# A two-layer decode kernel: VectorE turns x and q between the layers, an eleventh K tile stays in SBUF, and the pieces around the turn are cut anew

## The chip, the cores and the metric

The kernel runs on 1 core of one Trainium2 chip. The time is device microseconds of one execution; of several runs the median is given. The profile is of one execution.

## The reference

Two identical layers of decoding for B = 4 rows of D = 512 floats. Each layer is attention over a cache (32 query heads in 8 groups of 4, 4096 cached positions of 128 floats), then a gated feed-forward of width 1792. Everything is fp32. Both layers use the same cache and the same weights.

```python
x = A_x
for _ in range(2):
    h = layernorm(x)                        # (h - mean) / sqrt(var + 1e-5)
    q = (h @ wq).reshape(4, 1, 32, 128)     # 4 query heads to each of 8 cache heads
    p = softmax(q @ k_cache.T * 128 ** -0.5)
    x = x + (p @ v_cache).reshape(4, 1, 4096) @ wo
    h = layernorm(x)
    x = x + (silu(h @ w1) * (h @ w3)) @ w2
```

## The kernel before, in words

**Tiles.** For one cache head the K and V of all four rows are cut into 32 tiles of 128 partitions by 4 KB (0.524 MB each): tiles 0 to 15 are K (two halves of eight), 16 to 31 are V (two halves of eight). A head is done in four stages on TensorE: `score` of the first half (L391, two matmuls a tile), `score` of the second, `weigh` of the first half of V (L450, two matmuls a tile), `weigh` of the second. DVE takes the maxima (L403), ACT the exponentials (L407), TensorE turns the result (L414). The output of one head is turned and multiplied by its part of wo during the next head's first scores (`turn_o` after four tiles, `gather_o` after six).

**Order of the heads.** Layer 0 takes heads 0 to 7, layer 1 takes 7 to 0. Head 7 is thus used twice in a row, and a part of it stays in SBUF over the feed-forward: the K tiles in `KEPT` (6 to 15), and of tiles 0 and 1 three quarters, which ACT puts into three PSUM banks (`stored`) and back.

**The ring.** `space` holds 216 KB in each partition. wq and wo of all heads lie at fixed places from 96 KB up (`at_wq`, `at_wo`; 8 KB each) and are given back head by head in layer 1 (`vacate`). All else is a ring, handed out when the program is built: `plan` lists the pieces in the order of their transfers, `pump` issues the next piece as soon as `take` finds a place for it, and `done` gives a piece's place back when the last of its tiles has been read, in the program's order. `take` is first-fit: the lowest hole that is long enough, between the two limits that `narrow` sets. One piece needs one hole in one stretch. The plan is strictly in order: a piece that finds no place holds up all behind it.

```python
for i, (at, size) in enumerate(free):
    a, b = max(at, low, limit[0]), min(at + size, limit[1])
    if b - a >= n:
```

On the chip the issue (SP, L217; L205 for weights at fixed places, L215 for the rest of tile 1) waits by semaphores for the reads and the earlier transfers of those bytes. Transfers take eight semaphores in turn (DMAHW0 to DMAHW7).

`PARTS` says how many tiles each piece of K and V has, for every layer and head. For layer 1 these are: head 6 (3, 2, 2, 5, 4, 7, 9), head 5 (10, 8, 7, 7), head 4 (7, 1, 13, 11), and so on; a piece of 10 tiles is 40 KB in each partition.

**The turn.** At the end of layer 0, w1 lies at 0 to 28 KB (two pieces, L205), the kept tiles above it, wq and wo above 96 KB, and w3, w2 and the first pieces of layer 1 pass through what is left: 28 to 56 KB, a ring of 28 KB. Between w2's last matmul (L567) and the first score of layer 1 the chain is: add x and sum its rows (DVE, L581), mean (TensorE, L308), turn x (TensorE, L316 and L317; ACT copies, L320), q = x wq (L352, which also gives wq's place back), scale by 1/std (DVE, L356; the power by GpSimd, L332), turn q (TensorE, L357), lay it out (DVE, L342).

Of the kernel before, what the change touches and what calls it, by code (L numbers as in the profile page):

```python
# [14 lines left out]
LAYERS = 2  # L15
# [36 lines left out]
TURN = HKV - 1  # L52
KEPT = range(6, 16)
STORED = 0
# [4 lines left out]
PARTS = [{0: (16, 16), 1: (16, 16), 2: (16, 16), 3: (10, 7, 7, 8), 4: (16, 9, 7), 5: (8, 10, 7, 7), 6: (11, 13, 8),  # L59
# [4 lines left out]


W2_PARTS = ((0, 2), (2, 4), (4, 6), (6, 8), (8, 10), (10, 12), (12, 13), (13, 14))
BUSY = (4, 1, 2, 2, 1)
# [7 lines left out]
def tile_decode_layers(ctx: ExitStack, tc: tile.TileContext, x, kv, wqo, wo0, w1, w3, w2, out):  # L75
# [58 lines left out]
    def keep(at, n, src, given=None):  # L134
        plan.append((None, src, (at, n, (at, n) if given is None else given)))
# [16 lines left out]
    def w1_load():  # L152
        for k, n in ((0, 3), (3, 1)):
            keep(k * F // KB, n * F // KB, w1[:, k * F:(k + n) * F])

# [3 lines left out]
    for layer in range(LAYERS):  # L159
# [26 lines left out]
        for u in range(2):  # L186
            for k in (0, 2):
                a = 4 * KC * FW[0] * u + 4 * FW[u] * k
                stream([("w3", layer, u, k), ("w3", layer, u, k + 1)], w3[:, a:a + 8 * FW[u]])
        for a, b in W2_PARTS:  # L190
            stream([("w2", layer, a)], w2[:, a * D:b * D])

# [63 lines left out]
    nc.vector.tensor_scalar(same, same, -1.0 / D, None, op0=ALU.mult)  # L256
    spare = const.tile([P, 1], F32, name="spare")
    half = const.tile([P, 1], F32, name="half")
    nc.vector.memset(half, -0.5)


# [48 lines left out]

    def layernorm(xin, rowsum):
        busy(BUSY[2])
        pt = turned()
        at = [o_ps[1][:, i:i + 1] for i in range(2)]
        mean(at[0], rowsum)
        nc.tensor.matmul(pt[:, 0, :], xin, ident, start=True, stop=False)  # L316
        nc.tensor.matmul(pt[:, 0, :].rearrange("p (k c) -> p k c", k=KC), rowsum.to_broadcast([P, P]),  # L317
                         same.rearrange("p (k c) -> p k c", k=KC), start=False, stop=True)
        xT = work.tile([P, P], F32, name="xT", bufs=1)
        nc.scalar.activation(xT, pt[:, 0, :], AF.Copy)  # L320
        xc = work.tile([P, P], F32, name="xc", tag="tmp", bufs=1)
        nc.vector.tensor_scalar(xc, xin, at[0], None, op0=ALU.add)
# [3 lines left out]
        rstd = small("rstd")  # L326

        def factor():
            mean(at[1], ssq)
            ve = small("ve")  # L330
            nc.vector.tensor_scalar(ve, at[1], EPS, None, op0=ALU.add)
            nc.gpsimd.tensor_tensor(rstd, ve, half, op=ALU.pow)  # L332

        return xT, rstd, factor

# [9 lines left out]
    def wq_of(g):  # L345
        return place(at_wq(g), HOME).rearrange("p (k n) -> p k n", k=KC)

    def project_q(layer, g, xT, rstd):
        w = wq_of(g)
        for k in range(KC):  # L350
            for h in range(REP):
                nc.tensor.matmul(misc[32 * h:32 * h + 32, :], xT[:, 32 * k:32 * k + 32],  # L352
                                 w[:, k, h * DH:(h + 1) * DH], start=(k == 0), stop=(k == KC - 1))
        vacate(at_wq(g))
        q = work.tile([P, DH], F32, name="q", tag="tmp", bufs=1)
        nc.vector.tensor_scalar(q, misc, rstd, SCALE, op0=ALU.mult, op1=ALU.mult)  # L356
        nc.tensor.transpose(misc, q, ident)  # L357
        copy_q(misc.rearrange("p (h b) -> p b h", h=REP)[:, 0:B, :])

# [41 lines left out]

    def maximum(i, ps, acc):
        nc.vector.tensor_reduce(acc[:, i:i + 1], ps, axis=AX.X, op=ALU.max, negate=True)  # L403

    def exponent(i, ps, acc):
        p = work.tile([P, NT, P], F32, name="p", bufs=1)
        nc.scalar.activation(p.rearrange("p n s -> p (n s)"), ps, AF.Exp, bias=acc[:, i:i + 1],  # L407
                             accum_out=acc[:, 2 + i:3 + i])
        return p
# [103 lines left out]

    def feed_forward(layer, xT, rstd, factor, rowsum):
        pg = o_ps[0]
# [17 lines left out]
        gate = work.tile([P, FJ], F32, name="gate", tag="p", bufs=1)  # L533
        nc.scalar.activation(gate, pg[:, 0:FJ], AF.Sigmoid, scale=rstd)
        nc.scalar.activation(spare, half, AF.Exp)
        nc.vector.scalar_tensor_tensor(gate, pg[:, 0:FJ], rstd, gate, op0=ALU.mult, op1=ALU.mult)
        pt = turned()

        def hidden(u):
            s = slice(FW[0] * u, FW[0] * u + FW[u])  # L540
            nc.vector.scalar_tensor_tensor(gate[:, s], sides[u][:, 0:FW[u]], rstd, gate[:, s], op0=ALU.mult, op1=ALU.mult)

# [19 lines left out]
        def down():  # L562
            for i, (a, b) in enumerate(W2_PARTS):
                t = loaded("w2", layer, a).rearrange("p (n e) -> p n e", n=b - a)
                for m in range(a, b):
                    for k in range(KC):
                        nc.tensor.matmul(x_ps[32 * k:32 * k + B, :], hT[:, m, :],  # L567
                                         t[:, m - a, k * P:(k + 1) * P], start=(m == 0), stop=(m == 13))
                done("w2", layer, a)
                if i == 0:  # L570
                    turn_h(1)

        up(0, range(KC))
        hidden(0)
        up(1, (0, 1))
# [3 lines left out]
        down()  # L579
        if layer < LAYERS - 1:  # L580
            nc.vector.scalar_tensor_tensor(x_sb, x_ps, 1.0, x_sb, op0=ALU.mult, op1=ALU.add,  # L581
                                           accum_out=rowsum)
        else:
            nc.vector.tensor_tensor(x_sb, x_ps, x_sb, op=ALU.add)

    rowsum = small("rowsum")
    nc.vector.reduce_sum(rowsum, x_sb, axis=AX.X)
    for layer in range(LAYERS):
        xT, rstd, factor = layernorm(x_sb, rowsum)
        order = orders[layer]  # L590
        factor()
        if layer:
            project_q(layer, order[0][0], xT, rstd)
        else:
            share_q(layer, order[0][0], xT)
            turn_q(take_q(rstd))
            copy_q()

        ready = HKV - 3 if layer == 0 else HKV - 2
        between = {}  # L600
        for n, (g, (first, last)) in enumerate(order):
            acc = work.tile([P, 24], F32, name="acc")
            ps = score(layer, g, first, between)
            maximum(0, ps, acc)
            if n + 1 < len(order):
                share_q(layer, order[n + 1][0], xT)
            p = exponent(0, ps, acc)
            pT = turn(p)
            between = {}
            if n + 1 < len(order):  # L610
                shares = take_q(rstd)
                between[2] = lambda shares=shares: turn_q(shares)
            if n > ready:
                between[4] = lambda n=n: add_o(take_o(gathered if n == ready + 1 else wide))
            ps = score(layer, g, last, between)
            maximum(1, ps, acc)
            p = exponent(1, ps, acc)
# [10 lines left out]
        nc.scalar.activation(spare, half, AF.Sigmoid)  # L628
# [5 lines left out]
        xT, rstd, factor = layernorm(x_sb, rowsum)  # L634
        rowsum = small("rowsum")
        feed_forward(layer, xT, rstd, factor, rowsum)
    nc.sync.dma_start(out, x_sb)

# [43 lines left out]
```

## Time and profile before

| | |
|---|---|
| median of 3 runs | 709.15 us (708.6 to 709.89) |
| the profiled execution | 707.68 us |
| its span | 705.9 us |
| read from HBM | 298.65 MB, 423 GB/s over the span |
| busy: TensorE, VectorE, ScalarE, GpSimd | 61%, 20%, 6%, 0% of the span |
| mean granted TensorE clock | 0.823 |

The span is the profiled part of the execution; 1.8 us lie around it. "SPq" rows are issues of transfers. In a row of the timeline the two numbers ahead are start and length in us; the bracket behind is how long the engine had been idle before it, and what ended that. fp32 matmuls stand as two instructions each (x32 is 16 matmuls), and two matmuls on different column groups run side by side.

### The profile page before, as it was taken

The numbers are of one execution on the slowest core, as the hardware profiler recorded it, in microseconds if no ns is written. First come the engines' busy times: TensorE is split into PE (matmuls) and PEld (weight loads), VectorE is DVE, ScalarE is ACT, GpSimd is POOL, SyncE is SP. The second block draws the span as 40 slices with busy tenths as digits, with TensorE's granted clock in tenths as the row PEclk, the third lists the DMA queues.
The fourth block names the chain that finished last, engine by engine and source line by source line (L and its number), as shares of the span: only waits on it lengthen the run. The fifth ranks groups of instructions, "written<-read, shape, count | busy, mean of one in ns | idle before, by whom it ended". The sixth has DMA issues, their size and how long they took to land.

```text
span 705.9 us, 7248 instructions
## 1 busy us (share of the span) xinstructions
PE 431.1 (61%) x3161; PEld 134.6 (19%) x3161; DVE 142.1 (20%) x500; ACT 42.4 (6%) x101; POOL 2.9 (0%) x10
## 2 busy tenths in 40 slices
PE   3515734648526677466777857585386573566777
PEld 2101201212102122121224212121121121121223
DVE  3102102103201213031121301212112121212231
ACT  0000000100001000001111101010000101000011
POOL 0000000000000000000000000000000000000000
PEclk9977767859868769798899978799768987788898
DMA  9999999999999999999999999999999999999997
GB/s 420 416 417 431 450 420 418 467 411 424 452 408 431 443 420 431 446 413 424 424 412 411 403 430 440 429 426 431 437 431 435 422 451 428 442 428 412 421 419 279
DMA packets 15151, 299.18 MB, mean 424 GB/s; under 512 B 1680, under 2 KB 1936, under 8 KB 5392
## 3 DMA queue, kind: packets, MB, share of 16 engines
q1 hardware_dynamic: 14976, 298.65, 99.1%
q8 instruction: 25, 0.41, 0.2%
q10 hardware_dynamic: 144, 0.07, 0.0%
q14 instruction: 6, 0.05, 0.0%
HBM read 298.65 MB, written 0.07 MB: 423 GB/s over the span
## 4 chain that ended last, share of the span: by engine, by line
DMA 74%; PE 21%; another core or an unknown queue 2%; DVE 1%; ACT 1%; issue 1%; SPq 0%; ACTq 0%; DVEq 0%
DMA space<-in_kv 67%; PE scores L391 11%; DMA space<-in_w 8%; PE o L450 6%; PE sums_ps L375 1%; PE stored L501 1%; PE turned L414 1%; ACT p L407 1%; DVE acc L403 0%; PE sums_ps L567 0%; PE sums_ps L473 0%; PE o L523 0%; PE scores L300 0%; PE sums_ps L352 0%
## 5 line engine op out<-in xcount | busy, mean ns | idle before, releaser
L391 PE MATMUL scores<-space,qT 128*32 128x512 f32 x1024 | 176.2, 737 | 119.2 <-DMA space<-in_kv 118.7
L450 PE MATMUL o<-space,pT 128*16 128x512 f32 x1024 | 156.0, 706 | 118.4 <-DMA space<-in_kv 108.9
L391 PEld LDWEIGHTS scores<-space,qT 128*32 128x32 f32 x1024 | 37.0, 126 | 203.5 <-issue 185.1
L450 PEld LDWEIGHTS o<-space,pT 128*16 128x16 f32 x1024 | 31.5, 108 | 222.4 <-DMA space<-in_kv 125.8
L407 ACT ACTIVATE p<-scores,acc 128x512 f32<-128x512 f32 x32 | 22.0, 687 | 575.9 <-DVE acc L403 442.3
L403 DVE TENSOR_REDUCE acc<-scores 128x1 f32<-128x512 f32 x32 | 22.1, 691 | 156.0 <-PE scores L391 151.4
L416 DVE COPY pT<-turned 128x256 f32<-128x256 f32 x32 | 13.6, 424 | 186.8 <-PE turned L414 186.8
L463 DVE SCALAR_TENSOR_TENSOR o<-o,acc,o 128x128 f32<-128x128 f32 x112 | 39.3, 351 | 43.3 <-PE o L450 39.9
L414 PE MATMUL turned<-ident,p 128*128 128x128 f32 x128 | 23.5, 312 | 13.2 <-ACT p L407 13.2
L474 DVE COPY oT<-sums_ps 128x16 f32<-128x16 f32 x16 | 2.8, 174 | 109.0 <-PE sums_ps L473 109.0
L414 PEld LDWEIGHTS turned<-ident,p 128*128 128x128 f32 x128 | 15.0, 153 | 45.3 <-ACT p L407 28.0
L363 PE MATMUL sums_ps<-space,xT 128*32 128x512 f32 x120 | 19.1, 656 | 2.9 <-DMA space<-in_wqo 2.7
L375 PEld LDWEIGHTS sums_ps<-same,shares 128*128 128x128 f32 x120 | 17.0, 218 | 16.6 <-DVE shares L370 9.4
L375 PE MATMUL sums_ps<-same,shares 128*128 128x4 f32 x120 | 18.3, 276 | 1.0 <-DVE shares L370 1.0
L501 PE MATMUL stored<-space,oT 128*32 128x512 f32 x104 | 14.4, 593 | 0.0
L567 PE MATMUL sums_ps<-space,hT 128*4 128x128 f32 x224 | 9.5, 285 | 5.4 <-DMA space<-in_w 5.4
L370 DVE TENSOR_SCALAR shares<-sums_ps,rstd 128x512 f32<-128x512 f32 x15 | 11.1, 743 | 2.0 <-PE sums_ps L363 2.0
L473 PEld LDWEIGHTS sums_ps<-head,o 128*128 128x128 f32 x32 | 6.0, 233 | 22.0 <-issue 18.3
L523 PE MATMUL o<-space,xT 128*32 128x192 f32 (+1 forms) x128 | 7.3, 356 | 3.2 <-DMA space<-in_w 3.2
L300 PE MATMUL scores<-ident 128*128 128x256 f32 (+2 forms) x22 | 8.1, 451 | 1.4 <-POOL ident masks.py:199 1.4
L473 PE MATMUL sums_ps<-head,o 128*128 128x16 f32 x32 | 7.6, 314 | 1.2 <-DVE o L463 1.2
L529 PE MATMUL o<-space,xT 128*32 128x448 f32 x64 | 6.8, 545 | 1.1 <-DMA space<-in_w 0.7
(95 smaller groups left out, 135.3 us busy)
## 6 DMA issues: line engine op xcount, KB each, us to landing
space<-in_kv SPq DMA_DIRECT2D x11, 3584.0 KB, 20.7
space<-in_kv SPq DMA_DIRECT2D x7, 4096.0 KB, 22.2
space<-in_kv SPq DMA_DIRECT2D x4, 5632.0 KB, 22.9
space<-in_kv SPq DMA_DIRECT2D x4, 5120.0 KB, 20.0
space<-in_kv SPq DMA_DIRECT2D x14, 1024.0 KB, 11.5
space<-in_kv SPq DMA_DIRECT2D x2, 6656.0 KB, 23.7
space<-in_wqo SPq DMA_DIRECT2D x3, 4096.0 KB, 39.5
space<-in_kv SPq DMA_DIRECT2D x2, 4608.0 KB, 18.0
```

What stands on the lines that cost most here:

```text
L363: nc.tensor.matmul(wide[32 * k:32 * k + 32, :], xT[:, 32 * k:32 * k + 32], w[:, k, :], start=True, stop=True)
L370: nc.vector.tensor_scalar(shares, wide, rstd, -D * SCALE, op0=ALU.mult, op1=ALU.mult)
L375: nc.tensor.matmul(misc[:, h * B:(h + 1) * B], shares[:, h * DH:(h + 1) * DH], same[:, 0:B], start=True, stop=True)
L391: nc.tensor.matmul(ps[32 * b:32 * b + 32, :], qT[:, b, at:at + 32], t[:, i * BLOCK:(i + 1) * BLOCK], start=(m < 2), stop=(m >= TILES - 2))
L403: nc.vector.tensor_reduce(acc[:, i:i + 1], ps, axis=AX.X, op=ALU.max, negate=True)
L407: nc.scalar.activation(p.rearrange("p n s -> p (n s)"), ps, AF.Exp, bias=acc[:, i:i + 1], accum_out=acc[:, 2 + i:3 + i])
L414: nc.tensor.transpose(pt[:, n, :], p[:, n, :], ident)
L416: nc.vector.tensor_copy(pT, pt.rearrange("p n (b r) -> p n b r", b=B)[:, :, :, 0:ROW])
L450: nc.tensor.matmul(o_ps[i][32 * b:32 * b + ROW, :], pT[:, r // 2, b, :], t[:, j * NB * DH:(j + 1) * NB * DH], start=(r < 2), stop=(r >= TI ...
L463: nc.vector.scalar_tensor_tensor(o, o_ps[s][:, j * DH:(j + 1) * DH], acc[:, 16 + NB * s + j:17 + NB * s + j], o, op0=ALU.mult, op1=ALU.add)
L473: nc.tensor.matmul(misc[:, 0:B * REP], o, head, start=True, stop=True)
L501: nc.tensor.matmul(bank[32 * h:32 * h + 32, :], oT[:, h, :], w[:, h, :], start=first, stop=last)
```

## The change

- `KEPT` is tiles 5 to 15: eleven K tiles of head 7 (44 KB) stay over the turn, and layer 1 loads 0.524 MB less. The ring at the turn is 28 to 52 KB: 24 KB.
- Head 7's pieces in both layers are cut anew, finer in V and at the start of layer 1. The lists of all other heads are as before.
- w1 comes as 20 and 8 KB (21 and 7 before). At the turn w3's first half comes in four pieces of 4 KB (two of 8), its second half in two of 6 KB as before. At the end of layer 1 w3 comes in two pieces (16 and 12 KB; four before) and w2 in five (8, 8, 6, 4, 2 KB; eight before).
- At the turn DVE turns x straight from PSUM (in blocks of 32 by 32; the rows of wq, w1 and w3 are laid out to match) and turns q; x is added to w2's sums by a matmul with the identity; the scaling by 1/std is left to the scores of that head (`maximum` and `exponent` take a scale). So that q needs no mean, wq of head 7 is centred in place during head 5 of layer 0 (`center`: four matmuls and one DVE add).

```diff
-KEPT = range(6, 16)
+KEPT = range(5, 16)
...
-          7: ((6, 28), (2, 28), (8, 28), (2, 24), (6, 0), (4, 32), (2, 32), (2, 24))},
+          7: ((5, 32), (3, 52), (8, 64), (2, 20), (5, 0), (1, 28), (4, 32), (1, 48), (2, 20), (1, 28))},
...
-          7: (((2, 2), 2), ((3,), 24), None, ((1, 2, 2), 27), ((2, 2, 2, 2), 16))}]
-W2_PARTS = ((0, 2), (2, 4), (4, 6), (6, 8), (8, 10), (10, 12), (12, 13), (13, 14))
+          7: (((2, 1), 2), ((2, 1), 24), None, ((1, 2, 2), 27), ((2, 2, 2, 2), 16))}]
+W1_PARTS = (20, 8)
+W3_PARTS = (((1, 1, 1, 1), (2, 2)), ((4,), (4,)))
+W2_PARTS = ((2, 2, 2, 2, 2, 2, 1, 1), (4, 4, 3, 2, 1))
...
+    def lay_down(xin):
         xT = work.tile([P, P], F32, name="xT", bufs=1)
-        nc.scalar.activation(xT, pt[:, 0, :], AF.Copy)
+        nc.vector.transpose(xT, xin)
+        return xT
...
+    def center(g):
+        w = wq_of(g)
+        for k in range(KC):
+            nc.tensor.matmul(stored[1], share.to_broadcast([P, P]), w[:, k, :], start=(k == 0), stop=(k == KC - 1))
+        nc.vector.tensor_tensor(w, w, stored[1].unsqueeze(1).to_broadcast([P, KC, REP * DH]), op=ALU.add)
+    def turn_over(g):
+        busy(BUSY[2])
+        xT = lay_down(x_ps)
+        rowsum = small("rowsum")
+        nc.scalar.activation(x_sb, x_ps, AF.Copy, accum_out=rowsum)
+        w = wq_of(g).rearrange("p k (h i c) -> p k i h c", h=REP, i=KC)
+        for k in range(KC):
+            for i in range(KC):
+                nc.tensor.matmul(misc[32 * i:32 * i + 32, :].rearrange("p (h c) -> p h c", h=REP),
+                                 xT[:, 32 * k:32 * k + 32], w[:, k, i], start=(k == 0), stop=(k == KC - 1))
+        vacate(at_wq(g))
+        q = work.tile([P, P], F32, name="q", tag="tmp", bufs=1)
+        nc.vector.transpose(q, misc)
...
```

SP's issues at the end of layer 0, from the last V pieces of head 7 to w3 (the columns are floats in a row: 1024 are 4 KB), before:

```order
L217 DMA space<-in_kv 128x4096
L217 DMA space<-in_kv 128x2048 x2
L205 DMA space<-in_w 128x5376
L205 DMA space<-in_w 128x1792
L217 DMA space<-in_w 128x2048 x2
L217 DMA space<-in_w 128x1536 x2
```

and after:

```order
L225 DMA space<-in_kv 128x4096
L225 DMA space<-in_kv 128x1024
L225 DMA space<-in_kv 128x2048
L225 DMA space<-in_kv 128x1024
L213 DMA space<-in_w 128x5120
L213 DMA space<-in_w 128x2048
L225 DMA space<-in_w 128x1024 x4
L225 DMA space<-in_w 128x1536 x2
```

The same bytes go in smaller pieces. SP's issues in layer 1 from head 6's 28 KB piece (7168 floats: V tiles 16 to 22) to head 5's last, with the semaphores that each waits for; before:

```order
L217 DMA space<-in_kv 128x7168 [waits DMAHW4_49,DMAHW1_49,PE_49]
L217 DMA space<-in_kv 128x9216 [waits DMAHW6_49,DMAHW7_49,DMAHW5_49,PE_49]
L217 DMA space<-in_kv 128x10240 [waits DMAHW1_49,PE_49]
L217 DMA space<-in_kv 128x8192 [waits DMAHW2_49,DMAHW0_49,PE_49]
L217 DMA space<-in_kv 128x7168 [waits DMAHW3_49,PE_49]
L217 DMA space<-in_kv 128x7168 [waits PE_49]
```

and after:

```order
L225 DMA space<-in_kv 128x7168 [waits DMAHW6_49,DMAHW1_49,PE_49]
L225 DMA space<-in_kv 128x9216 [waits DMAHW3_49,DMAHW4_49,DMAHW0_49,PE_49]
L225 DMA space<-in_kv 128x10240 [waits DMAHW5_49,DMAHW7_49,DMAHW2_49,PE_49]
L225 DMA space<-in_kv 128x8192 [waits DMAHW6_49,PE_49]
L225 DMA space<-in_kv 128x7168 [waits PE_49]
L225 DMA space<-in_kv 128x7168 [waits DMAHW0_49,PE_49]
```

The pieces and their order are the same; what moved is their places in the ring, and with them the transfers and reads that each waits for. The piece of 10240 floats (40 KB) signals DMAHW3 before and DMAHW0 after, and the piece ahead of it the semaphore one lower. DVE at the turn, from the last copy of the feed-forward to the first maximum of layer 1, before:

```order
L558 COPY hT<-turned 64x8 x2
L581 SCALAR_TENSOR_TENSOR x_sb,rowsum<-sums_ps,x_sb 128x128
L322 TENSOR_SCALAR xc<-x_sb,o_117 128x128
L325 SCALAR_TENSOR_TENSOR sq,ssq<-xc 128x128
L331 TENSOR_SCALAR ve<-o_117 128x1
L356 TENSOR_SCALAR q<-sums_ps,rstd 128x128
L342 COPY qT<-sums_ps 128x4x2x4
L403 TENSOR_REDUCE acc<-scores 128x1
```

and after:

```order
L604 COPY hT<-turned 64x8 x2
L329 STREAM_TRANSPOSE xT<-sums_ps 128x128
L377 STREAM_TRANSPOSE q<-sums_ps 128x128
L379 TENSOR_SCALAR qT<-q 128x4x2x4
L324 TENSOR_SCALAR xc<-x_sb,o_117 128x128
L329 STREAM_TRANSPOSE xT<-xc 128x128
L335 SCALAR_TENSOR_TENSOR sq,ssq<-xc 128x128
L341 TENSOR_SCALAR ve<-o_117 128x2
L447 TENSOR_REDUCE acc<-scores 128x1
```

The work on the mean and the variance moved behind q.

More of the change, by code (lines that the diff above doesn't have):

```diff
@@ L308, in mean, with deviation, squares @@
         nc.tensor.matmul(out, same, part, start=True, stop=True)
[L311 to L318, printed above, removed]
+    def deviation(rowsum):
+        at = o_ps[1][:, 0:1]
+        mean(at, rowsum)
+        xc = work.tile([P, P], F32, name="xc", tag="tmp", bufs=1)
+        nc.vector.tensor_scalar(xc, x_sb, at, None, op0=ALU.add)
+        return xc
+    def lay_down(xin):
         xT = work.tile([P, P], F32, name="xT", bufs=1)
-        nc.scalar.activation(xT, pt[:, 0, :], AF.Copy)
-        xc = work.tile([P, P], F32, name="xc", tag="tmp", bufs=1)
-        nc.vector.tensor_scalar(xc, xin, at[0], None, op0=ALU.add)
+        nc.vector.transpose(xT, xin)
+        return xT
+    def squares(xc):
         sq = work.tile([P, P], F32, name="sq", tag="p", bufs=1)
@@ L325, in layernorm, with inverse @@
         nc.vector.scalar_tensor_tensor(sq, xc, -1.0, xc, op0=ALU.mult, op1=ALU.mult, accum_out=ssq)
-        rstd = small("rstd")
-        def factor():
[L329 to L332, printed above, removed]
+        return ssq
+    def inverse(out, var):
+        n = out.shape[-1]
+        ve = work.tile([P, 2], F32, name="ve", bufs=1)
+        nc.vector.tensor_scalar(ve[:, 0:n], var, EPS, None, op0=ALU.add)
+        nc.gpsimd.tensor_tensor(out, ve[:, 0:n], half[:, 0:n], op=ALU.pow)
@@ new lines, in turn_over, with factor @@
+    def turn_over(g):
[11 more added lines that the diff above has]
+        nc.vector.transpose(q, misc)
+        q = q.rearrange("p (h b) -> p b h", h=REP)[:, 0:B, :]
+        nc.vector.tensor_scalar(qT[:, :, LEAD:].rearrange("p b (t r) -> p b t r", t=2)[:, :, :, 0:REP],
+                                q.unsqueeze(2).to_broadcast([P, B, 2, REP]), SCALE, None, op0=ALU.mult)
+        xc = deviation(rowsum)
+        xT = lay_down(xc)
+        ssq = squares(xc)
+        rstd = work.tile([P, 2], F32, name="rstd", bufs=1)
+        def factor():
+            mean(o_ps[1][:, 1:2], ssq)
+            for b in range(B):
+                nc.tensor.matmul(o_ps[1][32 * b:32 * b + 32, 2:3], same[:, b:b + 1].to_broadcast([P, 32]), ssq,
+                                 start=True, stop=True)
+            inverse(rstd, o_ps[1][:, 1:3])
@@ L346, in wq_of @@
         return place(at_wq(g), HOME).rearrange("p (k n) -> p k n", k=KC)
[L348 to L358, printed above, removed]
     def share_q(layer, g, xT):
@@ L562, in down @@
         def down():
[L563 to L570, printed above, removed]
+            for m in range(14):
+                t = loaded("w2", layer, m)
+                for k in range(KC):
+                    nc.tensor.matmul(x_ps[32 * k:32 * k + B, :], hT[:, m, :], t[:, k * P:(k + 1) * P],
+                                     start=False, stop=(m == 13))
+                done("w2", layer, m)
+                if m == 1:
                     turn_h(1)
         up(0, range(KC))
+        nc.tensor.matmul(x_ps, ident, x_sb, start=True, stop=False)
         hidden(0)
@@ L603, in tile_decode_layers @@
             ps = score(layer, g, first, between)
-            maximum(0, ps, acc)
+            scale = rstd[:, 1:2] if layer and n == 0 else None
+            maximum(0, ps, acc, scale)
             if n + 1 < len(order):
                 share_q(layer, order[n + 1][0], xT)
-            p = exponent(0, ps, acc)
+            p = exponent(0, ps, acc, scale)
             pT = turn(p)
@@ L610, in tile_decode_layers @@
             if n + 1 < len(order):
-                shares = take_q(rstd)
+                shares = take_q(rstd[:, 0:1])
                 between[2] = lambda shares=shares: turn_q(shares)
+            if layer == 0 and n == TURN - 2:
+                between[6] = lambda: center(TURN)
             if n > ready:
```

101 lines of the change are left out of this document (58 added, 43 removed).

## The prediction

> **What bounds the kernel now.** I read the page first, then busy time by stretch, then who waits for whom, and last the timeline of the second layer. The page (busy shares, tenths per slice, DMA queue, chain of work that ended last):
>
> ```profile
> PE 431.1 (61%) x3161; PEld 134.6 (19%) x3161; DVE 142.1 (20%) x500; ACT 42.4 (6%) x101; POOL 2.9 (0%) x10
> DMA  9999999999999999999999999999999999999997
> q1 hardware_dynamic: 14976, 298.65, 99.1%
> DMA 74%; PE 21%; another core or an unknown queue 2%; DVE 1%; ACT 1%; issue 1%; SPq 0%; ACTq 0%; DVEq 0%
> ```
>
> No compute engine is over 61% busy, the DMA engines are busy in all slices but the last, and 74% of the last chain is transfers. Busy time by stretch (the last two columns are the DMA share and GB/s): the two layers' attention, the turn between them, and two pieces of the turn in which mostly w2 with rows of 4 KB moves.
>
> ```profile
> 10.00:350.00 340.00, 190.99 (x1258) 56.10 (x1258) 60.31 (x202) 17.94 (x45) 0.00 (x0) 0.80 1.00 430
> 350.00:390.00 40.00, 29.31 (x386) 13.65 (x382) 9.44 (x39) 4.25 (x8) 1.10 (x2) 1.00 1.01 408
> 395.00:690.00 295.00, 191.68 (x1285) 55.85 (x1288) 62.26 (x219) 15.79 (x41) 0.24 (x1) 0.81 1.00 430
> 370.00:376.00 6.00, 4.73 (x75) 2.92 (x67) 1.11 (x4) 0.00 (x0) 0.00 (x0) 1.00 1.02 408
> 376.00:382.00 6.00, 3.21 (x83) 1.69 (x82) 0.40 (x3) 0.00 (x0) 0.00 (x0) 1.00 1.04 409
> 396.00:402.00 6.00, 6.00 (x54) 1.66 (x47) 1.48 (x6) 1.07 (x3) 0.00 (x0) 1.00 1.01 425
> ```
>
> So the time is bytes over rate, and an edit counts if it changes the bytes or lets the queue run dry. What can let it run dry is SP: a piece is issued only when its place in the ring is free, that is when TensorE has read what lay there. The margin is what is still queued at an issue. Two places of the second layer show it, in the timeline of SP (an issue each) and of TensorE:
>
> ```profile
> 440.41 0.33 SPq L217 DMA_DIRECT2D space<-in_kv  x1
> 454.63 0.33 SPq L217 DMA_DIRECT2D space<-in_kv  x1
> 490.88 0.33 SPq L217 DMA_DIRECT2D space<-in_kv  x1
> 436.76 3.61 PE L450 MATMUL o<-space,pT 128*16 128x512 f32 x28 [3.15 <-DMA space<-in_kv]
> 447.53 1.90 PE L450 MATMUL o<-space,pT 128*16 128x512 f32 x4 [7.16 <-DMA space<-in_kv]
> 486.42 5.28 PE L450 MATMUL o<-space,pT 128*16 128x512 f32 x28 [3.61 <-DMA space<-in_kv]
> 495.05 1.92 PE L391 MATMUL scores<-space,qT 128*32 128x512 f32 x16 [3.35 <-DMA space<-in_kv]
> ```
>
> At 440.41 the 40 KB piece (head 5, tiles 0 to 9) goes out; the piece before it (36 KB, head 6, V tiles 23 to 31) lands at 447.5, when TensorE starts on it. So the queue still holds 7.1 us. At 490.88 the 52 KB piece of head 4 goes out 4.2 us before the first seven tiles of head 4 land (495.05), with tile 7 behind them.
>
> **Part 1, one tile less.** 0.524 MB at 430 GB/s: **-1.2 us**.
>
> **Part 2, piece sizes.** Finer at the turn: five K and V tiles and the first half of w3, 4.7 MB, move in rows of 4 KB at 408 instead of 425 GB/s: +0.45. Coarser at the end: eleven tiles of w2, 2.9 MB, from 409 to 425 (-0.3), and w3, 3.7 MB, from 425 to 430 (-0.1). Sum **0.0**, bounds -0.5 and +0.5.
>
> **Part 3, the chain at the turn.** From the last matmul of w2 to the first score (the timeline of DVE, ACT, TensorE and SP), with the rows that bound the new steps (DVE's transpose of 32 columns, its copy of 256) and the stretch with the dip:
>
> ```profile
> 382.90 0.29 DVE L581 SCALAR_TENSOR_TENSOR x_sb<-sums_ps,x_sb 128x128 f32<-128x128 f32 x1 [6.49 <-PE sums_ps L567]
> 384.67 1.08 PE L352 MATMUL sums_ps<-space,xT 128*32 128x128 f32 x32
> 385.81 0.33 SPq L215 DMA_DIRECT2D space<-in_kv  x1
> 386.91 3.64 PE L391 MATMUL scores<-space,qT 128*32 128x512 f32 x32 [0.28 <-DVE qT L342]
> 342.75 0.21 DVE L422 STREAM_TRANSPOSE rows<-acc 128x32 f32<-128x32 f32 x1
> 351.35 0.42 DVE L416 COPY pT<-turned 128x256 f32<-128x256 f32 x1 [7.94 <-PE turned L414]
> 388.00:392.00 4.00, 3.41 (x32) 0.78 (x24) 0.69 (x1) 0.63 (x2) 0.00 (x0) 1.00 0.95 336
> ```
>
> Before, 4.0 us pass from 382.90 to 386.91. After: a transpose of 128 columns, taken as 0.3 (between 0.21 and 0.42), 1.08 of matmuls, another 0.3, a scaling of 0.2 to 0.3 and gaps: 2.1 us. TensorE gains 1.9 us, and wq's place (the issue at 385.81) comes free about 1.4 us earlier. This pays only where DMA runs dry. The one dip is 336 GB/s from 388 to 392, which is 4 x (430 - 336) / 430 = 0.9 us; but its share stays 0.95, so most engines still had work. Gain between 0 and -0.9; I take **0**, since the ring is also 4 KB smaller (the third rival). The last add becoming a copy is 0.29 us against about the same: 0.
>
> **Part 4, centring wq in layer 0.** Four matmuls of 512 columns with 128 weights, one of which took 1.13 us with its drain (some 0.9 in a row), plus one DVE add over 2048 columns: 3.5 us more on TensorE in the second scores of head 5. Behind them waits the issue at 270.25; the piece issued before it ran until 276.68 (chain of waits):
>
> ```profile
> 357.11 1.13 PE L300 MATMUL scores<-ident 128*128 128x512 f32 x2
> 270.25 0.33 SPq L217 DMA_DIRECT2D space<-in_kv  x1
> 254.22 22.46 DMA space<-in_kv
> ```
>
> Cover 6.4 us, need 3.5 and about 1.3 of start-up: **0**. DVE's add delays only the second maximum; TensorE has 16 weighing matmuls before it needs that.
>
> **Part 5, the places in the second layer.** The sizes of heads 6 to 0 in the second list are kept, but the kept tiles are 44 KB instead of 40, so the first-fit allocator puts these pieces elsewhere. Walking the plan through `take` and `give` (KB of the ring, start-end):
>
> Before, when the 40 KB piece is due: the 36 KB piece lies at 44-80, the 28 KB piece (V tiles 16 to 22) at 84-112, wq 6 is free to 120. When V tile 22 is read, 80-120 is free: exactly 40. After: the 36 KB piece is at 52-88, so the hole is 88-120, 32 KB; below, 28-52 is 24 KB. Neither holds 40. It fits when the 36 KB piece is given back, goes to 28-68, and lies over tiles 23 to 26 of that piece: it waits until that piece has landed and six second-half matmuls have read tile 26 (SP's rows with the change show it: the 40 KB piece now waits for three earlier landings, the one just before it too). In before the 32 KB piece at 28-60 waits for the very same matmul, and was issued at 454.63. **Stall 1**: 454.63 - 447.53 = 7.1, plus start-up of the empty queue.
>
> Start-up: the output's 64 KB landed 1.5 us after issue, 0.15 of it its bytes at 430 GB/s: 1.3.
>
> ```profile
> out<-x_sb SPq DMA_DIRECT2D x1, 64.0 KB, 1.5
> ```
>
> So stall 1 is **+8.4 us**, bounds 7.1 (no start-up) and 8.7.
>
> The Trainium skill, page "DMA: Bandwidth & Descriptors", section "Anatomy of one DMA", gives each transfer some 2.0 us beside its bytes; by that estimate both stalls together would be 1.4 us longer. The output's row has 1.5 in all, and I go by it.
>
> The 52 KB piece: before, head 4's first seven tiles are at 28-56 and tile 7 at 144; 56-108 is free once V tile 29 of head 5 is read. After, the seven tiles lie at 56-84 and tile 7 at 128-132: holes 28-56 and 84-128 (28 and 44 KB). It goes to 28-80 only when the seven are scored, and waits for tile 5's second matmul, the twelfth of head 4. With only tile 7 (0.524 MB, 1.2 us) behind them in the queue, **stall 2** is twelve scores + 1.3 - 1.2. Twelve scores as in before, with the turning of o in between, at full clock and (head 3) at half clock:
>
> ```profile
> 496.91 0.40 PE L473 MATMUL sums_ps<-head,o 128*128 128x16 f32 x2
> 497.23 1.07 PE L391 MATMUL scores<-space,qT 128*32 128x512 f32 x8
> 539.37 3.64 PE L391 MATMUL scores<-space,qT 128*32 128x512 f32 x16 [6.79 <-DMA space<-in_kv]
> 543.48 1.50 PE L391 MATMUL scores<-space,qT 128*32 128x512 f32 x8
> ```
>
> 495.05 to 498.30 is 3.3; 539.37 to 544.98 is 5.6. TensorE's pause ahead of them should be like the 3.35 of before, since the same two 28 KB pieces follow each other; that pause left the clock full (eight scores in 1.92), while 6.79 halved it (3.64). So 3.3: **+3.4 us**, bounds 2.1 and 5.7.
>
> The Trainium skill, page "TensorE: Matmul & The Clock Gate", section "What's actually happening", halves the clock after an idle window of about 3.4 us that does not start with the kernel; 3.35 stands at that edge, so by it the half-clock case, +2.3, is open, and the row of 495.05 shows the full one.
>
> Later pieces keep their margin, and from the last piece of head 3 on the places are the old ones.
>
> **The sum.** -1.2 + 0 + 0 + 0 + 8.4 + 3.4 = +10.6. The profiled execution took 707.68 with a span of 705.9; the median of the runs shown is 709.15, 1.5 above. So 718.3 for an execution like it, and **719.8** for the median.
>
> **Rivals.**
> 1. *Only the first stall*: the hole for the 52 KB piece exists after all, or more than tile 7 is queued then. 709.15 - 1.2 + 8.4 = 716.4. For it: stall 2 rests on a longer walk of places. Chance 0.08.
> 2. *The old margin holds* (the other side): the 40 KB piece finds its place when V tile 22 is read, as at 440.41 in before, 7.1 us ahead of need; both stalls go and the tile's bytes are left: 709.15 - 1.2 = 708.0, at best 707.1 with the dip. It turns on 40 KB of hole at that moment; I count 32. Chance 0.05.
> 3. *The turn runs dry too*: with 24 KB, w3's second half cannot be issued until the first matmuls on w3 have run, where before all four pieces went out together. Those matmuls and the ones on the next piece (timeline of TensorE):
>
> ```profile
> 367.30 1.07 PE L523 MATMUL o<-space,xT 128*32 128x256 f32 x16 [1.01 <-DMA space<-in_w]
> 369.69 1.07 PE L523 MATMUL o<-space,xT 128*32 128x256 f32 x16 [1.31 <-DMA space<-in_w]
> ```
>
> The issue would come by 367.9 and the queue lasts to 369.7: 1.8 us for a start-up of 1.3, and the smaller first piece lands earlier still. If TensorE is late, 1 to 3 us more: 720.8 to 722.8. Chance 0.08.
>
> The forecast (both stalls, the turn fed) keeps 0.79.
>
> **How the numbers follow.** Low end 715.5: one stall only (716.4), with the dip gained. High end 724.5: half clock in stall 2 (+2.3) and the turn dry (+1 to 3) on 719.8. Outside lie the second rival and the joint mishaps, under 2 in 10. About 0.2%, 1.4 us, is what a measurement of this kernel tells from no change. Faster by more needs the second rival with part of the dip: 0.04; within it 0.01; slower 0.95.
>
> **What would show it.** Right: the page's DMA row shows two slices of layer 2, near 450 and 505 us, below 9; SP's waits put the 40 KB piece behind TensorE's L496, some 7 us after the landing before it; the 52 KB piece behind L435; HBM read falls by 0.52 MB; from the last w2 matmul to the first score about 2 us. Wrong: a DMA row of nines throughout, or the stalls in the turn instead.

## The result and the profile after

| | before | after |
|---|---|---|
| median | 709.77 us (6 runs, 708.60 to 710.93) | 730.12 us (6 runs, 725.16 to 732.13) |
| ratio, 95% interval | | 1.0274 (1.0246 to 1.0302) |
| the profiled execution, its span | 707.68, 705.9 us | 730.09, 727.6 us |
| read from HBM | 298.65 MB | 298.12 MB |

The change costs 20.35 us; 719.8 was forecast, with a range up to 724.5. The sign and the two stalls came as forecast, the size did not. The page of after, in the rows that answer to those of before (tenths per slice, GB/s per slice, the data queue, the last chain):

```profile
DMA  9999999999999999999999997799699999999997
GB/s 407 404 458 409 453 425 422 447 416 433 431 421 428 445 417 410 438 430 416 420 346 366 423 439 304 288 416 424 270 449 436 413 441 436 450 414 421 431 415 304
q1 hardware_dynamic: 14976, 298.13, 96.5%
DMA 70%; PE 26%; another core or an unknown queue 2%; DVE 1%; issue 1%; ACT 0%; SPq 0%; ACTq 0%; DVEq 0%
```

Counted from 0, slices 24 and 25 (437 to 473 us) and slice 28 (509 to 527) are the two stalls. But slices 20 and 21 (364 to 400 us), where the DMA row still shows nines, move only 346 and 366 GB/s. Busy time by stretch, four rows of before and then four of after (DMA share and GB/s in the last columns):

```profile
365.00:392.00 27.00, 19.00 (x286) 9.28 (x278) 4.47 (x16) 4.60 (x9) 0.55 (x1) 1.00 1.01 400
392.00:440.00 48.00, 35.62 (x234) 10.25 (x234) 10.40 (x35) 3.08 (x10) 0.00 (x0) 0.86 1.02 431
440.00:475.00 35.00, 23.63 (x144) 6.44 (x142) 7.22 (x24) 0.84 (x3) 0.00 (x0) 0.80 1.00 428
475.00:540.00 65.00, 35.64 (x226) 10.04 (x230) 12.89 (x48) 2.86 (x8) 0.00 (x0) 0.80 1.01 434
```

```profile
365.00:392.00 27.00, 20.27 (x270) 9.91 (x264) 3.80 (x14) 4.06 (x8) 0.40 (x1) 0.81 0.96 355
392.00:440.00 48.00, 36.00 (x238) 10.13 (x230) 11.04 (x37) 2.93 (x8) 0.70 (x1) 0.86 1.01 414
440.00:475.00 35.00, 13.26 (x72) 2.98 (x76) 4.97 (x20) 0.90 (x3) 0.00 (x0) 0.73 0.68 287
475.00:540.00 65.00, 39.79 (x248) 11.44 (x244) 9.81 (x31) 2.63 (x7) 0.00 (x0) 0.78 0.90 385
```

The missing GB/s, over 430: 27 x 45 / 430 = 2.8 us in the turn, 48 x 17 / 430 = 1.9 after it, 35 x 141 / 430 = 11.5 around the first stall, 65 x 49 / 430 = 7.4 around the second. That is 23.6, less the tile's 1.2: 22.4, against 21.7 between the spans. So there are three places: the turn, forecast at nothing, and the two stalls, forecast at 8.4 and 3.4. In this one execution all three are larger than forecast. What each is worth in time is measured by the runs below; for the first stall they give less than the 11.5 counted here.

The two stalls stand in the chain of waits of after, where transfers and TensorE take turns (start, length, what):

```profile
437.31 16.16 DMA space<-in_kv
...
453.51 1.89 PE o L496 x4
...
456.97 3.18 PE o L496 x14
...
460.17 14.47 DMA space<-in_kv
...
489.28 21.95 DMA space<-in_kv
...
511.37 3.28 PE scores L435 x16
514.64 0.33 PE sums_ps L519 x2
514.97 1.04 PE scores L435 x8
...
516.02 18.07 DMA space<-in_kv
```

The 36 KB piece lands at 453.47, TensorE reads tiles up to 26, the 40 KB piece goes out at 460.17. The 28 KB piece lands at 511.23, twelve scores are made, the 52 KB piece goes out at 516.02. In the chain of before transfers and TensorE take turns too, but the issues come while earlier transfers are still under way: the 40 KB piece is issued at 440.41, 7 us before the 36 KB piece lands, and the piece behind the 52 KB one at 500.08, before that one has landed.

```profile
440.41 19.20 DMA space<-in_kv
...
474.20 20.71 DMA space<-in_kv
...
500.08 25.83 DMA space<-in_kv
```

### The profile page after: what moved, and what is told of

It is laid out like the page before. It is cut to its first block, busy times and chain, and to the rows that moved or that the text cites. A ratio compares the mean times of both kernels' runs of the same rounds, so it can differ in the third digit from the quotient of the medians.

```text
span 727.6 us, 7260 instructions
## 1 busy us (share of the span) xinstructions
PE 437.7 (60%) x3162; PEld 135.0 (19%) x3162; DVE 145.5 (20%) x507; ACT 41.8 (6%) x99; POOL 3.1 (0%) x10
## 3 DMA queue, kind: packets, MB, share of 16 engines
HBM read 298.12 MB, written 0.07 MB: 410 GB/s over the span
## 4 chain that ended last, share of the span: by engine, by line
DMA 70%; PE 26%; another core or an unknown queue 2%; DVE 1%; issue 1%; ACT 0%; SPq 0%; ACTq 0%; DVEq 0%
DMA space<-in_kv 63%; PE o L496 11%; PE scores L435 9%; DMA space<-in_w 6%; PE turned L460 1%; PE sums_ps L419 1%; PE o L575 1%; PE stored L361 0%; DVE pT L462 0%; PE sums_ps L612 0%; ACT p L453 0%; DVE acc L447 0%; PE o L569 0%; PE stored L547 0%
## 5 line engine op out<-in xcount | busy, mean ns | idle before, releaser
L496 PE MATMUL o<-space,pT 128*16 128x512 f32 x1024 | 160.0, 721 | 113.6 <-DMA space<-in_kv 105.1
L569 PE MATMUL o<-space,xT 128*32 128x192 f32 (+1 forms) x128 | 9.6, 415 | 2.7 <-DMA space<-in_w 2.7
L309 PE MATMUL scores<-ident 128*128 128x128 f32 (+2 forms) x20 | 7.7, 469 | 0.0
## 6 DMA issues: line engine op xcount, KB each, us to landing
space<-in_kv SPq DMA_DIRECT2D x7, 4096.0 KB, 22.4
space<-in_kv SPq DMA_DIRECT2D x4, 2560.0 KB, 22.4
```

The lines of the kernel that those rows point to most:

```text
L496: nc.tensor.matmul(o_ps[i][32 * b:32 * b + ROW, :], pT[:, r // 2, b, :], t[:, j * NB * DH:(j + 1) * NB * DH], start=(r < 2), stop=(r >= TI ...
```

## The experiments

Theory: the places (part 5) make the two stalls, and the 24 KB ring costs something in the turn. Rival: the new turn itself makes TensorE late, and the stalls are that lateness handed on. Each run's ratio is to runs of the kernel before on the same chip. Of the long lists in `PARTS` the edits show only changed entries, each by its head's number; `...` stands for lines left out.

**Both stalls out.** Two sizes of head 5 in the second layer change places.

```diff
-5: (10, 8, 7, 7)
+5: (8, 10, 7, 7)
```

> The kernel after, with the first two pieces of head 5 in the second layer swapped (8 and 10 tiles instead of 10 and 8), so that the first finds the 32 KB hole as soon as head 6's 28 KB piece is read, and the 52 KB piece of head 4 finds its hole too. Places theory: both gaps in the transfers go. From the two traces, by last landings: the 40 KB piece cost 9.0 us, the slow piece after it 1.3, the 52 KB piece 5.2, so 730 - 15.5 = 714.5; what is left of the turn's 2.5 and of the 2.5 that the 36 KB piece lost stays: 712 to 716. Rival (TensorE comes late out of the turn, and any piece that waits for it is late by as much): one gap moves to another piece, and at most half of the 15.5 comes back: 720 to 726.

711.97 us against 709.35: 1.0028 (1.0006 to 1.0051). That is the lower end of what the places theory gave (712 to 716); the rival's 720 to 726 is out. One swap returns all but 2.6 us. The DMA row of its page is nines again:

```profile
DMA  9999999999999999999999999999999999999996
```

**The second stall out, the first kept.**

```diff
-4: (7, 1, 13, 11)
+4: (7, 1, 11, 13)
```

> The kernel after, with the last two pieces of head 4 in the second layer swapped (11 and 13 tiles instead of 13 and 11), so that the 44 KB piece finds a 44 KB hole while head 5's gap stays. Places theory: only the second gap goes, 5.2 us by last landings: 730 - 5.2 = 724.8 (723.5 to 726.5). If the second gap were an echo of the first (TensorE late), it would stay: 729 to 731.

720.42 us against 709.35: 1.018 (1.0124 to 1.0236; four runs, 717.9 to 725.5). The second stall goes and the first stays, as its DMA row shows, and an echo's 729 to 731 is out. But the time falls by more than the 5.2 us foreseen: 9.

```profile
DMA  9999999999999999999999999599999999999996
```

**The first stall out, the second kept.**

```diff
-5: (10, 8, 7, 7)
+5: (6, 4, 8, 7, 7)
```

> The kernel after, with the 40 KB piece of head 5 in the second layer cut into 24 and 16 KB (6 and 4 tiles): the 24 KB piece fits the hole that stood open, the first gap goes, and the places that follow still leave no hole for head 4's 52 KB piece. Stall 2 alone. Places theory: by last landings the 52 KB piece cost 5.2 us in after, on top of the run without both gaps (711.97): 717.2, within 715.5 to 719. Against the kernel with both gaps it is 9.0 + 1.3 and up to 2.5 of the slow engine's lag faster: 10.3 to 12.8. If the gaps were one chain of lateness, nothing of the second would be left: 711 to 713.

720.70 us against 709.48: 1.0144 (1.0111 to 1.0178). Above the range. The second stall is there as in after (chain of waits of this run):

```profile
504.85 3.29 PE scores L435 x16
...
509.52 18.07 DMA space<-in_kv
```

Taken as excess over the runs of before beside each, the kernel with no stall stands at 2.62, with the first alone at 11.07, with the second alone at 11.22, with both at 20.35. So the first stall is worth 8.5 (beside none) or 9.1 (beside the second), the second 8.6 or 9.3: they add, and neither is an echo of the other. Two more kernels with both stalls, further down, stood 18.9 (the old end) and 16.85 (fillers) above before, so the 20.35 of both may be too high by some us. Even by the least of them the second stall is worth 16.85 - 11.07 = 5.8, more than the 3.4 forecast.

**Only the new turn.** `turn_over`, `center` and the addition by TensorE, with ten kept tiles, the ring, the lists and the piece sizes of before.

```diff
-KEPT = range(5, 16)
+KEPT = range(6, 16)
...
-W1_PARTS = (20, 8)
-W3_PARTS = (((1, 1, 1, 1), (2, 2)), ((4,), (4,)))
-W2_PARTS = ((2, 2, 2, 2, 2, 2, 1, 1), (4, 4, 3, 2, 1))
+W1_PARTS = (21, 7)
+W3_PARTS = (((2, 2), (2, 2)), ((2, 2), (2, 2)))
+W2_PARTS = ((2, 2, 2, 2, 2, 2, 1, 1), (2, 2, 2, 2, 2, 2, 1, 1))
```

> The new turn alone (VectorE's transposes, wq centred in layer 0, x added by TensorE), with the ten kept tiles, the 28 KB ring, the lists and the piece sizes of before. Places and ring theory: the new turn itself costs nothing there; last w2 landing to first score is 3.4 us instead of 4.5, and the centring costs 0 to 1.0 in layer 0: 708.5 to 710.5. Rival (the new order of the turn makes the transfers run dry): the turn's loss of 2.5 to 3.7 us is here too: 712 to 713.5.

709.30 us against 709.35: 0.9992 (0.9972 to 1.0012). The rival is out: with the 28 KB ring the new turn costs nothing that these runs can tell.

**Only the eleventh tile, the 24 KB ring and the finer pieces,** with the old turn, the old end and the swap of the first run.

```diff
-KEPT = range(6, 16)
+KEPT = range(5, 16)
...
-5: (10, 8, 7, 7)
+5: (8, 10, 7, 7)
...
+W3_PARTS = (((1, 1, 1, 1), (2, 2)), ((2, 2), (2, 2)))
...
-        for k, n in ((0, 3), (3, 1)):
-            keep(k * F // KB, n * F // KB, w1[:, k * F:(k + n) * F])
+        for a, n in ((0, 20), (20, 8)):
+            keep(a, n, w1[:, a * KB:(a + n) * KB])
```

> The kernel before (its old turn, no centring, its old end), with the eleventh kept tile, the 24 KB ring, the finer w1 and w3 pieces and the lists of after, and with the same swap in head 5 as the run with both gaps taken out. Ring theory: the turn runs dry here as in after, 2.5 to 3.7 us with the tile's 1.2 already in it, so 711 to 714, within 1.5 us of the run with the new turn and the swap. Rival (the new turn is what runs dry): nothing is lost and the tile is gained: 707.5 to 709.

714.24 us against 709.35: 1.0062 (1.0037 to 1.0088). The loss comes with the tile, the ring and the pieces, not with the new turn. But the new turn, worth nothing with 28 KB, is worth 2.3 us with 24 (714.24 to 711.97, ten runs each, which spread over 5 to 6 us), more than the 1.5 allowed. That the shorter chain pays because the queue runs dry there is argued, not tested.

**The end's pieces as before,** in after.

```diff
-W3_PARTS = (((1, 1, 1, 1), (2, 2)), ((4,), (4,)))
-W2_PARTS = ((2, 2, 2, 2, 2, 2, 1, 1), (4, 4, 3, 2, 1))
+W3_PARTS = (((1, 1, 1, 1), (2, 2)), ((2, 2), (2, 2)))
+W2_PARTS = ((2, 2, 2, 2, 2, 2, 1, 1), (2, 2, 2, 2, 2, 2, 1, 1))
```

> The kernel after, with the w3 and w2 pieces at the end as before (two of 8 and two of 6 KB; six of 4 and two of 2 KB): both gaps are there, only the end is undone. It is also after once more, on the same chip as the other runs. From the last piece of head 4 to the end the two traces differ by 0.2 us (190.15 and 3.35 of after against 189.82 and 3.51 of before), so the coarse end is worth nothing: 728 to 732, as after. If the end's coarser pieces cost or gain, up to 2 us away from that.

728.38 us against 709.48: 1.0248 (1.0207 to 1.0288). No effect that these runs can tell.

**The new turn and the coarse end, with the ring, tiles and lists of before.**

```diff
-KEPT = range(5, 16)
+KEPT = range(6, 16)
...
-W1_PARTS = (20, 8)
-W3_PARTS = (((1, 1, 1, 1), (2, 2)), ((4,), (4,)))
+W1_PARTS = (21, 7)
+W3_PARTS = (((2, 2), (2, 2)), ((4,), (4,)))
```

> The new turn with the ten kept tiles, the 28 KB ring and all lists of before, and the coarse w3 and w2 pieces at the end: the change without the eleventh tile and without the smaller ring. By the run of the new turn alone (709.3) and no gain from the end: 708.5 to 710, the same as before. If the coarse end gains, 707 to 708.5, and this beats both kernels.

708.64 us against 709.48: 0.9992 (0.9972 to 1.0012). The same. **With the lists cut anew for that ring** (two entries shown; heads 7, 4 and 3, w1 and w2 are cut anew too):

```diff
-5: (10, 8, 7, 7)
+5: (10, 8, 8, 6)
...
-6: (3, 2, 2, 5, 4, 7, 9)
+6: (3, 4, 5, 4, 6, 1, 9)
```

> The new turn and the coarse end with the ten kept tiles and the 28 KB ring, as in the run before it, with the piece lists of the turn and of heads 6 to 3 in the second layer cut anew so that every piece finds its hole some microseconds earlier (w1 in 20 and 8 KB, w2 in nine pieces, head 6 in seven, head 5 as 10, 8, 8, 6, head 4 in five). If the old lists leave moments in which the slowest DMA engine's lag of 2 to 4 us empties the queue, they go: 707 to 708.5, faster than before. If the transfers are fed all the time already: 708.5 to 709.5, the same.

708.90 us against 710.24: 0.999 (0.9968 to 1.0012). Inconclusive: medians 0.8 and 1.3 us under before, both intervals across 1. No version here is shown to beat before.

**What the 24 KB ring wants.** First, w3 in before's 8 KB pieces, both stalls out:

```diff
-W3_PARTS = (((1, 1, 1, 1), (2, 2)), ((4,), (4,)))
+W3_PARTS = (((2, 2), (2, 2)), ((4,), (4,)))
```

> The kernel with the eleventh tile, the 24 KB ring and both gaps out (the run with head 5's pieces swapped, 711.97), with the first half of w3 at the turn in two pieces of 8 KB, as before, instead of four of 4 KB. Ring theory: the next piece waits for the matmuls on the first 8 KB instead of the first 4, one transfer of 0.5 MB (1.25 us) later, and again at the second: 1.3 to 2.7 us more, 713.2 to 714.7. If the finer pieces do nothing: 711.5 to 712.5.

712.66 us against 710.24: 1.0038 (1.0015 to 1.006). 2.4 above before, where the run with fine pieces was 2.6 above: the finer w3 buys nothing that these runs can tell, against my ring theory. Then w2 and heads 7 to 3 cut anew (two entries shown), with w3 in 4 KB pieces again:

```diff
-5: (8, 10, 7, 7)
+5: (2, 6, 6, 9, 9)
...
-7: (((2, 1), 2), ((2, 1), 24), None, ((1, 2, 2), 27), ((2, 2, 2, 2), 16))
+7: (((1, 1, 1), 2), ((1, 1, 1), 24), None, ((1, 2, 1, 1), 27), ((1, 1, 2, 2, 2), 16))
```

> The eleventh tile, the 24 KB ring, the new turn and the coarse end, with w2 and the pieces of heads 7 to 3 in the second layer cut anew (finer V pieces at the turn). Ring theory: the turn stays short of bytes in flight whatever the cuts, the 24 KB are the limit: 711 to 712.5, no better than the run with the swap alone (711.97) and behind the 28 KB ring (708.64). If the cuts were the cause: 708 to 709.5.

710.66 us against 710.24: 1.001 (0.9988 to 1.0032). Better than the 711 of the ring theory, short of the 709.5 that the cuts alone were to give: by medians the cuts are 2.2 of the 2.6 us, and 2.0 against the run with coarse w3 beside it. What stays stands in the stretch 365 to 392 of three runs: the 28 KB ring with the coarse end, the swap alone, these cuts:

```profile
365.00:392.00 27.00, 20.02 (x291) 9.53 (x283) 4.81 (x17) 4.44 (x9) 0.70 (x1) 0.94 1.02 410
```

```profile
365.00:392.00 27.00, 20.30 (x271) 10.08 (x267) 3.83 (x15) 4.06 (x8) 0.55 (x1) 0.81 0.95 354
```

```profile
365.00:392.00 27.00, 21.03 (x276) 10.48 (x269) 3.95 (x15) 4.06 (x8) 0.70 (x1) 0.81 0.98 369
```

410 GB/s with 28 KB, 354 and 369 with 24: 2.6 us of missing bytes even at 369, 1.2 of them paid back by the tile. The step from 354 to 369 shows no gain of the cuts: the traced executions with the 24 KB ring, ten kernels, lie between 352 and 386 here. But all of them are below the four with 28 KB (400 to 412). Where the cuts' 2.2 us lie, these traces do not show. In the last two rows the granted clock (third from the right) falls too, to 0.81, so that TensorE's speed could be the cause as well as the places. **Fillers to hold the clock:**

```diff
                 done("w3", layer, u, k)
+                if layer == 0 and u == 0 and k < 3:
+                    busy(2)
```

> The run with the eleventh tile, the 24 KB ring and the lists cut anew (710.66, 0.4 above the kernel before beside it), with a filler matmul of 256 columns after each of the first three w3 chunks of the turn, in TensorE's waits of 0.4 to 0.6 us. In that run's trace the granted clock fell to 0.50 from 370 to 376 us, w3's second half ran at half speed, and the transfers fell to 254 GB/s in 370 to 372. Clock theory: with the waits filled the clock stays at 1.00, the pieces behind it are issued sooner, and the turn gains up to 1 us: 0.5 below the kernel before to 0.1 above it. Ring theory: the transfers wait for places, not for TensorE's speed, and the fillers change nothing: 0.2 to 0.8 above the kernel before.

710.66 us against 709.73: 1.0012 (0.999 to 1.0034). The turn from 365 to 378 without the fillers, then with them:

```profile
365.00:378.00 13.00, 10.86 (x114) 5.56 (x107) 2.09 (x7) 2.12 (x3) 0.00 (x0) 0.74 0.94 356
```

```profile
365.00:378.00 13.00, 9.99 (x112) 4.95 (x104) 2.19 (x7) 2.12 (x3) 0.00 (x0) 1.00 0.97 365
```

The clock is at 1.00, the rate gains 9 GB/s of the 55 missing, the time nothing. Other traces agree: three kernels with the 24 KB ring kept the clock at 1.00 in this stretch without these fillers and moved 330, 345 (the run of the old end) and 369 GB/s. So TensorE's speed is not what the transfers lack; that they wait for places is what is left.

**Two fillers ahead of head 4's scores** (the expectation speaks of one), in after, against the half clock in the second stall:

```diff
+            if layer and n == 3:
+                busy(4)
+                busy(4)
             ps = score(layer, g, first, between)
```

> The kernel after, both gaps in, with one filler matmul of 512 columns ahead of head 4's first scores in the second layer, so that TensorE does not stand still for 3.3 us there. Clock theory: the sixteen matmuls that took 3.28 us at half clock in after take 1.92 as in before; the 52 KB piece is issued 1.4 us sooner after the landing it waits for, and the second gap is 1.4 us shorter: 728 to 729.5 where after has 730.1. If the clock has no part in it, the sixteen stay at 3.3 and the time at 729.5 to 731.

727.09 us against 710.24: 1.0239 (1.0199 to 1.0279). Below both ranges, but the edit missed its aim, so the clock's part in the time stays untested: the fillers ran as soon as TensorE was free, TensorE still stood 2.79 us behind them, and the sixteen scores ran at half clock again.

```profile
504.90 2.31 PE L309 MATMUL scores<-ident 128*128 128x512 f32 x4
510.00 3.15 PE L435 MATMUL scores<-space,qT 128*32 128x512 f32 x16 [2.79 <-DMA space<-in_kv]
```

## Why the prediction was wrong

By medians above before, step by step (new turn and coarse end alone, plus tile and ring, plus first stall, plus second): -0.84, 2.62, 11.07, 20.35. The terms of the sum beside that:

| step | forecast | measured |
|---|---|---|
| parts 1, 2, 3: tile, pieces, turn (ring of 24 KB) | -1.2 | +3.5 (2.62 + 0.84) |
| parts 3 and 4 with the old ring; end's pieces | 0 | -0.8, not told from 0 |
| part 5, first stall | +8.4 | +8.5 (9.1 the other way) |
| part 5, second stall | +3.4 (2.1 to 5.7) | +9.3 (8.6 the other way) |

The row of +3.5 is for the lists of after with the swap. With w2 and heads 7 to 3 cut anew, the same ring stands at +1.3 (0.42 + 0.84). So by medians not all of it is the ring's.

**The walk of the places held,** and both stalls stand where and for the reason forecast. That the first also has its forecast size is in part luck. In after TensorE's work behind the landing took 6.7 us (453.47 to 460.17), not 7.1, and the empty queue 2.3, not 1.3. Thirteen of the 16 DMA engines were also dry 2.7 us or more before the landing. That the stall let the slowest catch up (they landed 3.3 us apart before it, 0.5 behind it) may have paid for that; no run tests it.

**The turn (part 3, and the third rival at 0.08) failed.** I set 1.8 us of cover against a start-up of 1.3, took the turn as fed and put its term at 0. SP and TensorE in after, then two stretches of busy time:

```profile
367.69 0.33 SPq L225 DMA_DIRECT2D space<-in_w  x1
369.47 0.64 PE L569 MATMUL o<-space,xT 128*32 128x256 f32 x8 [1.69 <-DMA space<-in_w]
370.76 1.08 PE L569 MATMUL o<-space,xT 128*32 128x256 f32 x8 [0.64 <-DMA space<-in_w]
373.99 1.51 PE L569 MATMUL o<-space,xT 128*32 128x192 f32 x16 [0.16 <-DMA space<-in_w]
384.56 3.08 PE L612 MATMUL sums_ps<-space,hT 128*4 128x128 f32 x48 [2.46 <-DMA space<-in_w]
390.38 1.06 PE L435 MATMUL scores<-space,qT 128*32 128x512 f32 x8 [0.51 <-DVE qT L379]
```

```profile
366.00:368.00 2.00, 1.78 (x21) 0.57 (x13) 0.00 (x0) 0.53 (x1) 0.00 (x0) 1.00 0.92 365
368.00:370.00 2.00, 0.53 (x8) 0.16 (x8) 0.68 (x1) 1.59 (x3) 0.00 (x0) 1.00 0.74 209
```

The issue came at 367.69 as forecast, but its bytes landed at 373.85, 6.2 us later. The piece ahead of it landed at 371.97, so by landings the cover was 4.3 us, more than I had counted; yet the queue ran dry, at 209 GB/s in the next 2 us. In the trace the first of the 16 DMA engines had finished that piece at 367.91, 0.2 us behind the issue. In before, at the like issue (367.99), the first engine still had work for 2.6 us, and the stretch 368 to 370 moved 422 GB/s. The third rival was no alternative to the stalls but came on top of them, and I should have put its case into the sum: its upper price, 3 us, was still under the 4.7 that the runs give without the tile's gain (3.5 + 1.2).

**The chain itself (part 3)** was right in kind: from w2's last matmul (387.64) to the first score 2.7 us, 4.0 before, 2.1 forecast. VectorE's transposes of 128 columns took 0.32 us (0.3 forecast). `center` took 3.70 us of TensorE (3.5 forecast) and did not show.

**The second stall's size failed** in three pieces, all visible in after. The sixteen scores took 3.28 instead of 1.92: the half-clock case, which I had priced in the bounds and left out of the sum, +1.4. I had chosen full clock by one row, a wait of 3.35 us; here the wait was 3.32 (the last part says what decided). The 52 KB piece took 18.07 from issue to landing where its 6.82 MB need 15.9 at 430 GB/s: 2.2, not 1.3, +0.9; so too the 40 KB piece, 14.47 for 12.2. And the 1.2 us that tile 7 was to hide were not there: when TensorE was released, at 511.37, with tile 7 still to land, hardly a byte moved any more (stretches of after).

```profile
508.00:510.00 2.00, 0.04 (x2) 0.00 (x0) 1.40 (x4) 0.00 (x0) 0.00 (x0) 1.00 0.81 336
510.00:512.00 2.00, 0.64 (x4) 0.23 (x8) 0.00 (x0) 0.00 (x0) 0.00 (x0) 0.68 0.21 84
```

Together 3.4 + 1.4 + 0.9 + 1.2 = 6.9. The medians' 9 I cannot split further: with four to ten runs that spread over 4 to 8 us, a difference of two medians is sure to about 2, in my estimate.

Behind the turn and tile 7 lies the same fact: a landing is the landing of the slowest of 16 engines. At 510.67 the first engine was done with tile 7, at 512.46 the last. The first stall shows it more clearly; stretches of after as it begins:

```profile
446.00:448.00 2.00, 1.83 (x16) 0.26 (x8) 0.00 (x0) 0.00 (x0) 0.00 (x0) 1.00 0.90 387
448.00:450.00 2.00, 0.00 (x0) 0.00 (x0) 0.00 (x0) 0.00 (x0) 0.00 (x0) 1.00 0.73 313
450.00:452.00 2.00, 0.00 (x0) 0.00 (x0) 0.00 (x0) 0.00 (x0) 0.00 (x0) 1.00 0.13 55
452.00:454.00 2.00, 0.49 (x2) 0.13 (x4) 0.00 (x0) 0.00 (x0) 0.00 (x0) 0.68 0.00 0
```

TensorE is released at 453.5, after 2 us at 55 GB/s and more at nothing. In the trace's landings of this 36 KB piece the first engine is done at 450.15, the last at 453.47. I counted a queue as fed until the landing; it is fed until the first engines are done. This made both margins shorter, in the turn and behind tile 7; how much of either miss in time it is, no run separates.

The Trainium skill, page "DMA: Bandwidth & Descriptors", section "Anatomy of one DMA", gives a transfer some 2.0 us beside its bytes, measured there for transfers that GpSimd issues; these go out from SP. The two rows of an empty queue come near (2.2 and 2.3), and the 1.5 us of the small output that I went by did not carry over.

## What to carry to other kernels

Where a ring is planned by hand, the piece lists belong to the places: moving the ring by 4 KB cost 18 us through lists that nobody had touched, and swapping two numbers gave nearly all of it back. Judge a queue's margin from the first engine that runs dry and charge an empty queue issue, start-up and lag together; when two margins are thin at once, add their prices instead of holding them against each other as rivals. A shorter chain of compute may be worth something only where the transfers run dry: here the same new turn gained 2.3 us with the 24 KB ring and nothing with 28.

## What the runs showed of the hardware

TensorE's clock did not go by the length of the last wait alone. In before sixteen scores ran at full clock (1.92) after a wait of 3.35 us, in after at half clock after 3.32. In the run with only the new turn they ran at full clock after 3.33 us, and at half after 2.26 (two rows of that run, then the one of after):

```profile
461.00 1.92 PE L435 MATMUL scores<-space,qT 128*32 128x512 f32 x16 [3.33 <-DMA space<-in_kv]
496.51 3.34 PE L435 MATMUL scores<-space,qT 128*32 128x512 f32 x16 [2.26 <-DMA space<-in_kv]
511.37 3.28 PE L435 MATMUL scores<-space,qT 128*32 128x512 f32 x16 [3.32 <-DMA space<-in_kv]
```

In the turn with the 24 KB ring and the new cuts it fell to 0.50 with no wait over 0.7 us since 363:

```profile
370.00:372.00 2.00, 1.51 (x17) 0.89 (x14) 0.48 (x1) 0.00 (x0) 0.00 (x0) 0.50 0.74 254
```

The Trainium skill, page "TensorE: Matmul & The Clock Gate", section "What's actually happening", lets the clock fall after an idle window of about 3.4 us. The length agrees with the steps described next, but these rows do not agree with "idle": the clock fell after shorter waits, and after stretches that were only partly idle.

The clock records of the 14 traces show what counts. The clock holds for steps of 3.41 us or whole multiples (930 of 941 stretches), which lie differently in each run, and a step's clock goes with how long TensorE was busy, by the profile's records, in the step before. From full clock it fell 464 times, always after a step with TensorE busy for less than 0.69 of it (19 times in 20 for less than 0.44); it held 1282 times, always after 0.40 or more. From half it came back 457 times, always after 0.75 or more. So a wait counts by how it lies on the steps. The 3.35 us of before fell on two steps, busy for 0.55 and 0.46, and the clock held; the 3.32 of after left one step (507.3 to 510.7) at 0.21, and the scores behind it ran at half. Between 0.40 and 0.69 both happened; what decides there stays open.
